# Two DMA queues for the first K weights, and a ScalarE square root for the first tile, at the start of a tuned attention and SwiGLU kernel

## The chip, the cores and the metric

One core of a Trainium2 chip. The metric is the device time of one execution in microseconds (us), lower is better; a kernel is run several times and the median is quoted. A ratio of two kernels is the mean time of the one's fast runs over the mean of the other's fast runs of the same rounds, so it is not quite the ratio of the quoted medians. A run counts as slow when it is over 1.5% above the fastest of its kernel. "Within noise" below always refers to the 95% interval of such a ratio, or to the spread of the same kernel between executions.

## The reference, cut to what matters

```python
xn = layernorm(x)                                   # x: 2048 tokens x 1024
q, k, v = split(xn @ wqkv)                          # wqkv: 1024 x 3072, 32 heads of 32
pq, pk = phi(q), phi(k)                             # phi(t) = where(t > 0, t+1, exp(t)) + 1e-6
kv  = sum over tokens of pk^T v                     # linear attention, not causal
s   = (pq kv) / (pq . sum pk) @ wo
g   = silu((silu(xn @ w_gate) * (xn @ w_up)) @ w_down)
out = x + s * g
```

The matrix products are nearly all of the time. What this case is about happens in the first ten microseconds: tile 0 (128 tokens) has to be loaded, normalised and transposed, and the first weights of K have to arrive, before TensorE can do anything useful.

## The kernel before: the parts concerned

The kernel is written as a list of operations, each with its engine, what it reads and writes, and an estimated duration. A planner (`schedule`) sorts them into one instruction stream for each engine; the stream is fixed when the kernel is built. Cuts are marked with `...`.

Tile 0 of x is loaded in two halves, one issued by SyncE and one by ScalarE (ACT). The weights all go out from SyncE:

```python
def wkv_load(w, j, k):            # w: 0 = K, 1 = V; j: half of the columns; k: half of the rows
    ap, r = kvblock(w, KB_OF[k, j])
    c0 = 1024 * (1 + w) + j * 512
    dma([], [r], ap, wqkv_v[:, 4 * k:4 * k + 4, c0:c0 + 512], dsem("wkv%d%d%d" % (w, j, k)), 512 * KB)
```

The order of the loads is tile 0, tile 1, then K (j=1, k=0), K (1, 1), K (0, 0), K (0, 1), tile 2, V (1, 0), V (1, 1), tile 3, V (0, 0), V (0, 1). I call the four K loads **blocks one to four** in this order, 512 KB each, and V (1, 0) the first V block.

The normalisation of one tile; in tiles 0 and 1 VectorE (DVE) writes the result in two halves:

```python
def ln_tile(i):
    ...
    oA = dve([...], [sA], lambda h: h.bn_stats(stats[:, j, 0, :], xa[:, 0:512]), 512)
    oB = dve([...], [sB], lambda h: h.bn_stats(stats[:, j, 1, :], xa[:, 512:1024]), 512)
    if i == 1:                                # tile 1's statistics wait for two steps of tile 0
        for o, q in zip((oA, oB), first):
            o.preds.add(q)
            q.succs.append(o)
    dve([sA, sB], [mvr], lambda h: h.bn_aggr(mv[:, j, :], stats[:, j, :, :]), 60)
    o0 = dve([mvr], [ver], lambda h: h.tensor_scalar(veps[:, j, :], mv[:, j, 1:2], EPS_LN, None, ALU.add), 60)
    if i == 0:
        first.append(o0)
    pool([ver, nh_r], [rsr], lambda h: h.tensor_tensor(rstd[:, j, :], veps[:, j, :], neg_half[:, :], ALU.pow), 0.56)
    ...
            o0 = dve([s.r, mvr, rsr], [...], lambda h, c=c: h.tensor_scalar(
                oa[:, c:c + n], xa[:, c:c + n], mv[:, j, 0:1], rstd[:, j, :], ALU.subtract, ALU.mult), n, 2.6)
    first.append(o0)
```

On TensorE (PE) the start is: 15 warm-up matmuls on zeros, eight transposes of tile 0, six small filler matmuls, four matmuls with block one, four with block two, eight transposes of tile 1, then blocks three and four and tile 1.

## Time and profile before

| what | value | from |
|---|---|---|
| median of three runs, their range | 712.48 us (711.99 to 712.89) | the times |
| span of the profiled execution | 710.5 us | the page |
| PE busy | 705.0 us, 99% | the page |
| transposes of tile 0 begin | 6.41 us | PE's timeline |
| PE starts on block one, block two, block three | 7.93, 9.33, 10.84 us | PE's timeline |
| last landing of block one, two, three, four | 7.79, 9.28, 10.79, 12.28 us | the landing records |
| last landing of the first V block | 14.48 us | the landing records |

How to read it: a DMA runs on 16 engines and each reports its landing separately, so a block has 16 landings and is usable at the last. The useful work of PE is fixed, and from 10.84 to 177 us it has almost no holes. So a landmark some way in measures what the start gains or loses. I use eight transposes near 125 us for this (called the transposes of the sums in the expectations below): the traces show 669 matmuls ahead of them, or 658 where 11 records are missing. In the kernel before they start at 124.96 us. (The chain of waits shows them 0.17 us later, 125.13, as it leaves out the overlap with the matmul ahead; some expectations use that reading.) The landmark does not tell the end of the kernel: after it PE has further holes, which differ between executions, and from PE's last matmul to the end of the span it takes 2.99, 3.69 and 3.00 us in three traces of this kernel, and up to 4.89 (e3).

### The profile page before, as it was taken

What the parts mean: (1) busy time and instruction counts of PE and PEld (TensorE: products, weight loads), DVE (VectorE), ACT (ScalarE), POOL (GpSimd) and SP (SyncE); (2) the same over time, 40 slices, a digit from 0 to 9 for tenths busy, and PEclk for the clock granted to TensorE, in tenths of its full rate; (3) what the DMA queues carried; (4) which work ended last, traced back from release to release, by engine and by line L of the source; (5) the groups of instructions that cost most, each with busy time, mean ns of one, the idle gap of its engine ahead of it and who ended that gap; (6) DMA issues with size and microseconds to landing.
All of it is one profiled execution on the core that took longest, in us unless ns stands there. A gap on an engine that the chain in (4) does not pass through costs nothing.

```text
span 710.5 us, 11436 instructions
## 1 busy us (share of the span) xinstructions
PE 705.0 (99%) x4181; PEld 388.5 (55%) x4181; DVE 631.4 (89%) x1533; ACT 423.3 (60%) x825; POOL 14.1 (2%) x35
## 2 busy tenths in 40 slices
PE   8999999999999999999999999999999999999997
PEld 4444445555555555556556455555555555565654
DVE  6999858989999999998958999999999999798863
ACT  4788765988679676664212157876886756531212
POOL 2111000000000000000000000000000000000000
PEclk9999999999999999999999999999999999999999
DMA  9744133346565353326498854323716241656663
GB/s 293 151 109 99 32 118 119 120 132 195 165 186 145 103 156 112 107 65 174 124 244 216 205 142 149 109 71 94 208 59 192 76 149 60 179 140 160 144 156 96
DMA packets 140871, 98.64 MB, mean 139 GB/s; under 512 B 34960, under 2 KB 137872, under 8 KB 140816
## 3 DMA queue, kind: packets, MB, share of 16 engines
q1 hardware_dynamic: 140528, 97.74, 49.5%
q8 instruction: 32, 0.52, 0.3%
q10 hardware_dynamic: 288, 0.20, 0.1%
q14 instruction: 23, 0.19, 0.1%
HBM read 77.59 MB, written 12.71 MB: 127 GB/s over the span
## 4 chain that ended last, share of the span: by engine, by line
PE 96%; DMA 2%; SPq 0%; DVE 0%; issue 0%; ACT 0%
PE ps L309 96%; DMA W<-in_B_w_up_dram 1%; DMA H<-in_A_wqkv_dram 1%; SPq L455 0%; DVE W L452 0%; PE ps L316 0%; DVE ps L452 0%; DVE TM L452 0%; SPq L757 0%; ACT TM L441 0%
## 5 line engine op out<-in xcount | busy, mean ns | idle before, releaser
L309 PE MATMUL ps<-X,W 128*128 128x512 f16 (+2 forms) x1372 | 288.7, 350 | 0.0
L441 ACT ACTIVATE TM<-ps 128x512 f16<-128x512 f32 (+3 forms) x386 | 202.6, 555 | 101.9 <-PE ps L309 99.0
L309 PE MATMUL ps<-H,W 128*128 128x512 f16 (+2 forms) x1096 | 218.2, 351 | 0.1
L309 PEld LDWEIGHTS ps<-X,W 128*128 128x128 f16 (+1 forms) x1372 | 132.4, 98 | 103.6 <-ACT H L441 1.0
L452 DVE TENSOR_TENSOR W<-W 128x1024 f16<-128x1024 bf16 (+5 forms) x412 | 183.1, 478 | 3.5 <-PE ps L309 2.1
L309 PEld LDWEIGHTS ps<-H,W 128*128 128x128 f16 (+1 forms) x1096 | 106.1, 98 | 94.8 <-DVE ps L452 0.6
L452 DVE TENSOR_TENSOR ps<-ps,TM 128x256 f32<-128x256 f32 (+1 forms) x250 | 131.5, 527 | 13.4 <-PE ps L309 10.0
L441 ACT ACTIVATE ps<-ps 128x512 f32<-128x512 f32 (+1 forms) x174 | 85.8, 494 | 90.3 <-PE ps L309 89.7
L441 ACT ACTIVATE H<-ps 128x512 f16<-128x512 f32 (+1 forms) x132 | 78.4, 606 | 38.3 <-PE ps L309 38.3
L309 PE MATMUL ps<-P,W 128*128 128x256 f16 (+1 forms) x516 | 99.5, 319 | 0.0
L452 DVE TENSOR_TENSOR H<-H 128x1024 f16<-128x1024 f16 (+5 forms) x126 | 71.2, 578 | 0.8 <-ACT H L441 0.4
L441 ACT ACTIVATE TM<-TM 128x512 f16<-128x512 f32 (+1 forms) x70 | 43.7, 630 | 45.5 <-DVE TM L452 45.3
L309 PEld LDWEIGHTS ps<-P,W 128*128 128x128 f16 (+1 forms) x516 | 50.2, 98 | 29.0 <-ACT TM L441 0.8
L309 PE MATMUL ps<-W 128*128 128x256 f16 (+1 forms) x330 | 61.8, 282 | 0.0
L452 DVE TENSOR_TENSOR H<-H,TM 128x512 f16<-128x512 f16 (+1 forms) x120 | 48.0, 417 | 8.5 <-ACT H L441 8.3
L452 DVE TENSOR_TENSOR TM<-ps,TM 128x512 f32<-128x512 f32 (+3 forms) x63 | 41.6, 660 | 13.6 <-PE ps L309 12.8
L309 PEld LDWEIGHTS ps<-W 128*128 128x128 f16 (+1 forms) x330 | 31.5, 98 | 31.7 <-DVE ps L452 1.2
L309 PE MATMUL ps<-H,X 128*128 128x512 bf16 (+1 forms) x150 | 35.0, 379 | 0.7 <-DMA H<-in_A_wqkv_dram 0.4
L452 DVE TENSOR_TENSOR TM<-TM 128x512 bf16<-128x512 f16 (+2 forms) x73 | 29.4, 412 | 6.4 <-ACT TM L441 4.5
L309 PE MATMUL ps<-H,P 128*128 128x512 bf16 (+1 forms) x110 | 26.8, 379 | 0.0
L452 DVE TENSOR_TENSOR H<-ps,TM 128x512 f16<-128x512 f32 (+1 forms) x35 | 24.0, 686 | 2.6 <-PE ps L309 1.7
L452 DVE TENSOR_TENSOR TM<-TM,W 128x512 f16<-128x512 f16 (+1 forms) x39 | 14.0, 363 | 11.5 <-ACT TM L441 11.4
(100 smaller groups left out, 397.7 us busy)
## 6 DMA issues: line engine op xcount, KB each, us to landing
W<-in_B_w_gate_dram SPq DMA_DIRECT2D x14, 1024.0 KB, 5.4
W<-in_B_w_up_dram SPq DMA_DIRECT2D x14, 1024.0 KB, 5.5
W<-in_B_w_down_dram SPq DMA_DIRECT2D x14, 896.0 KB, 6.2
H<-in_A_wqkv_dram SPq DMA_DIRECT2D x8, 512.0 KB, 8.1
H<-r_scratch SPq DMA_DIRECT2D x32, 128.0 KB, 3.8
W<-m_scratch SPq DMA_DIRECT2D x4, 1024.0 KB, 5.3
s_scratch<-TM SPq DMA_DIRECT2D x32, 128.0 KB, 2.0
TM<-in_A_x_dram SPq DMA_DIRECT2D x16, 256.0 KB, 3.5
```

The costliest lines, as they stand in the source:

```text
L309: last = h.matmul(o, l, r, start=st, stop=sp, skip_group_check=True)
L441: q = PL.op("act", reads, writes, lambda h: h.activation(o, i, func, **kw), nel(o) / (1000.0 if "bias" in kw or not isinstance(kw.get("sca ...
L452: return dve(reads, writes, lambda h: h.tensor_tensor(o, a, b, op), nel(o), 1.92 if fast else 0.96)
```

## The change

The intent: let the first weights land sooner by issuing two of the four K loads from ACT, and shorten the chain to tile 0's normalisation by replacing GpSimd's power with ACT's square root and VectorE's reciprocal. The core of the diff, shortened (`epsl` is a column filled with EPS_LN by VectorE at the start):

```diff
-        tab = ACT.Exp
+        tab = ACT.Sqrt                       # the planner's first activation table
...
         def wkv_load(w, j, k):
-            dma([], [r], ap, wqkv_v[...], dsem("wkv%d%d%d" % (w, j, k)), 512 * KB)
+            o = dma([], [r], ap, wqkv_v[...], dsem("wkv%d%d%d" % (w, j, k)), 512 * KB)
+            if (w, k) == (0, 0):             # K blocks one and three
+                beside.append(o)
...
-            o0 = dve([mvr], [ver], ... veps = var + EPS_LN ...)
             if i == 0:
+                o0 = act([mvr, el_r], [ver], veps[:, j, :], mv[:, j, 1:2], ACT.Sqrt, "sb", bias=epsl[:, :])
                 first.append(o0)
-            pool([ver, nh_r], [rsr], ... power ...)
+                dve([ver], [rsr], lambda h: h.reciprocal(rstd[:, j, :], veps[:, j, :]), 60)
+            else:
+                ... as before: veps on VectorE, power on GpSimd ...
...
                 for c in range(0, 1024, n):
-                    o0 = dve(... normalise half c ...)
+                    p0, o0 = o0, dve(... normalise half c ...)
+                    if c:
+                        o0.after = (p0,)     # second half of the normalisation behind the first
+                        p0.succs.append(o0)
...
         PL.schedule()
+        for o in beside:
+            o.eng = "act"
```

The queue is changed after planning, so the planner does not know of it. The Sqrt part does enter the plan.

More of the change, by code (lines that the diff above doesn't have):

```diff
@@ L375, in build_kernel @@
         epsc = sbt("epsc", [128, 1], F32)
+        epsl = sbt("epsl", [128, 1], F32)
         m_scr = nc.dram_tensor("m_scratch", [D, D], FP16)
@@ L569, in build_kernel @@
         wz = TM.at(0, 1 * KB, FP16)
+        el_r = named("el")
+        dve([], [el_r], lambda h: h.memset(epsl[:, :], EPS_LN), 60)
         wz_r = [TM.reg(0, KB // 4), TM.reg(KB // 4, 3 * KB // 4)]
@@ L762, in wkv_load @@
             c0 = 1024 * (1 + w) + j * 512
-            dma([], [r], ap, wqkv_v[:, 4 * k:4 * k + 4, c0:c0 + 512], dsem("wkv%d%d%d" % (w, j, k)), 512 * KB)
+            o = dma([], [r], ap, wqkv_v[:, 4 * k:4 * k + 4, c0:c0 + 512], dsem("wkv%d%d%d" % (w, j, k)), 512 * KB)
+            if (w, k) == (0, 0):
+                beside.append(o)
         xnslot = {}
-        first = []
+        first, beside = [], []
         def ln_tile(i):
@@ L779, in ln_tile @@
             dve([sA, sB], [mvr], lambda h: h.bn_aggr(mv[:, j, :], stats[:, j, :, :]), 60)
-            o0 = dve([mvr], [ver], lambda h: h.tensor_scalar(veps[:, j, :], mv[:, j, 1:2], EPS_LN, None, ALU.add), 60)
             if i == 0:
+                o0 = act([mvr, el_r], [ver], veps[:, j, :], mv[:, j, 1:2], ACT.Sqrt, "sb", bias=epsl[:, :])
                 first.append(o0)
-            pool([ver, nh_r], [rsr], lambda h: h.tensor_tensor(rstd[:, j, :], veps[:, j, :], neg_half[:, :], ALU.pow), 0.56)
+                dve([ver], [rsr], lambda h: h.reciprocal(rstd[:, j, :], veps[:, j, :]), 60)
+            else:
+                o0 = dve([mvr], [ver], lambda h: h.tensor_scalar(veps[:, j, :], mv[:, j, 1:2], EPS_LN, None, ALU.add), 60)
+                pool([ver, nh_r], [rsr], lambda h: h.tensor_tensor(rstd[:, j, :], veps[:, j, :], neg_half[:, :], ALU.pow), 0.56)
             o = xn_ring.take()
@@ L789, in ln_tile @@
                 for c in range(0, 1024, n):
-                    o0 = dve([s.r, mvr, rsr], [o.sub(2 * c, 2 * n).r], lambda h, c=c: h.tensor_scalar(
+                    p0, o0 = o0, dve([s.r, mvr, rsr], [o.sub(2 * c, 2 * n).r], lambda h, c=c: h.tensor_scalar(
                         oa[:, c:c + n], xa[:, c:c + n], mv[:, j, 0:1], rstd[:, j, :], ALU.subtract, ALU.mult), n, 2.6)
+                    if c:
+                        o0.after = (p0,)
+                        p0.succs.append(o0)
                 first.append(o0)
```

## The prediction

> **What bounds the kernel now.** I read the page first, for the busy shares and the chain that ended last; then that chain in order of time; then who waits; then the first 26 us engine by engine, because the chain sends me there.
>
> From the page (busy us, share, instructions), then three pieces of the chain in order of time (start us, us, what):
>
> ```profile
> PE 705.0 (99%) x4181; PEld 388.5 (55%) x4181; DVE 631.4 (89%) x1533; ACT 423.3 (60%) x825; POOL 14.1 (2%) x35
> PE 96%; DMA 2%; SPq 0%; DVE 0%; issue 0%; ACT 0%
> ...
> 2.20 7.09 DMA H<-in_A_wqkv_dram
> ...
> 10.84 114.29 PE ps L309 x624
> ```
>
> The tensor engine is busy 705.0 of 710.5 us, so 5.5 us is all that any change to waits can ever give back: 0.8% of the time. Stretch by stretch, PE lacks 1.8 us before 10.84, 0.14 us near 177 to 191, and 3.5 us in the tail after 705; elsewhere nothing. The change sits in the first stretch, so its direct worth is bounded by 1.8 us before anything else is said. The 1.04 us before PE's first instruction is not touched either.
>
> The waits of PE in the first 14 us (who, for whom, total, times, longest), then its own timeline there (start us, us, what, idle before):
>
> ```profile
> PE ps L309 <- DVE TM L571: 1.0, 1, 1.0
> PE ps L309 <- DMA H<-in_A_wqkv_dram: 0.4, 1, 0.4
> PE ps L309 <- ACT X L441: 0.3, 1, 0.3
> ```
>
> ```profile
> 1.04 5.30 PE L309 MATMUL ps<-TM 128*128 128x128 f16 x15 [1.04 <-DVE TM L571]
> 6.41 0.90 PE L316 MATMUL ps<-ident,W 128*128 128x128 f16 x8
> 7.14 0.50 PE L309 MATMUL ps<-TM 128*128 128x128 f16 x6
> 7.93 1.02 PE L309 MATMUL ps<-H,X 128*128 128x512 bf16 x4 [0.29 <-ACT X L441]
> 9.33 1.04 PE L309 MATMUL ps<-H,X 128*128 128x512 bf16 x4 [0.38 <-DMA H<-in_A_wqkv_dram]
> 10.21 0.61 PE L316 MATMUL ps<-ident,W 128*128 128x128 f16 x8
> ```
>
> The 15 warm-up matmuls are filler; real work begins with the transposes of tile 0 at 6.41 and runs without a hole from 10.84. Between lie the gaps that the change aims at. Matmuls of 512 columns start 0.215 us apart here, so the hole after the start at 8.58 is 9.33 - 8.80 = 0.53 us by starts (0.38 with modelled ends). After the transposes of tile 1 there is another of about 0.2 us, to 10.84.
>
> Matching each load's last landing with the instruction that waits for it gives the main point. The four K weight blocks (512 KB each; first columns-half 1 with k-half 0 and 1, then columns-half 0) land at 7.79, 9.28, 10.79 and 12.28; PE passes those waits at 7.82, 9.32, 10.83 and 13.22. The first V block lands at 14.48 and is waited for until 14.51, without a hole in the matmuls; the third V block lands at 18.17, wait passed at 18.20. So **the start is paced by one DMA stream to 18 us**, not only at the hole that the page shows.
>
> **What the Trainium skill says.** "DMA: Bandwidth & Descriptors", section "Issuing engines are not separate DMA queues": all issuing engines share the same 16 DMA engines, and a second issuer saves only issue time. The trace agrees that issue is small: SyncE's first weight issues take 0.43 to 0.64 us each, against 1.5 us between landings. The same page, "Queues, rings and completion order": each DMA engine takes turns between queues, packet by packet; the trace before has weights on one queue only, so no run shows it yet. "ScalarE: Activation LUTs", section "What ACT_TABLE_LOAD costs": 1283 ns for the load plus about 1380 ns of drain. The trace has eight loads of 1283 ns, but ACT's next instruction follows about 10 ns later (load 133.55, next 134.84): the drain is not seen as extra time, so I count 1.3 us. That section also gives 280 ns + 0.833 ns per element with a pointer bias; the trace's 128x128 activations take about 0.28 us.
>
> **The change, part by part.**
>
> (a) Standard deviation of tile 0. VectorE's and GpSimd's rows:
>
> ```profile
> 4.86 0.21 DVE L779 BATCH_NORM_AGGREGATE mv<-stats 128x2 f32<-128x12 f32 x1
> 5.11 0.15 DVE L780 TENSOR_SCALAR veps<-mv 128x1 f32<-128x1 f32 x1
> 5.35 0.56 POOL L783 TENSOR_TENSOR rstd<-veps,neg_half 128x1 f32<-128x1 f32 x1 [0.84 <-DVE veps L780]
> 5.94 0.73 DVE L790 TENSOR_SCALAR W<-W,mv,rstd 128x512 f16<-128x512 bf16 x2
> ```
>
> Today 5.07 to 5.94 = 0.87 us. New, an estimate: Sqrt with a pointer bias 0.28, reciprocal 0.17 (128x1 VectorE rows are 0.15, a small reciprocal elsewhere in the trace 0.20), three hand-offs of 0.03 to 0.04: 0.55 us. Saved 0.32. But PE is in order: its last warm-up starts at 5.70 and those start 0.43 apart, so PE is free only at 6.13, and the transposes can move from 6.41 to 6.13: **0.28 us at best**. A side effect goes the other way: half of tile 1's statistics ran free of charge in the power's shadow (5.30 to 5.98); now it falls behind the normalisation, and tile 1 may come 0.3 us later. That is covered if tile 0's matmuls on the third block stand beside it.
>
> (b) Table loads. The first load becomes Sqrt's, at the start where ACT idles to 6.84. A load for Exp is added, 1.3 us, after the four copies of tile 0 (end 8.16) and before the first Exp (10.40): 2.24 us idle there, so hidden with 0.9 us left. Worth 0.
>
> (c) Two queues. Issues now are at 1.73, 2.19, 2.74, 3.29. ACT is free at 1.18 after its half of x, so blocks one and three should go at about 1.2 and 1.65, and blocks two and four move up on SyncE to about 1.73 and 2.2: 0.5 to 1.1 us earlier. That is worth something only where the DMA engines had room. They had:
>
> ```profile
> 2.00:8.00 6.00, 5.64 (x26) 2.39 (x25) 3.99 (x10) 1.64 (x5) 2.72 (x12) 1.00 0.90 273
> 8.00:12.00 4.00, 3.60 (x22) 1.64 (x22) 2.58 (x6) 1.74 (x4) 0.34 (x1) 1.00 1.09 372
> ```
>
> The last two columns are the DMA share and GB/s. At 372 the first 6 us of traffic would take 4.4, so 1.6 us is the most that filling the stream gives. I count a third to a half, 0.5 to 0.8 us, as the low rate has a part that more queues need not mend: four of the 16 engines landed the first block at 7.71 to 7.79, ten by 5.8. Against it stands the turn-taking. In one queue block one ends after 1.0 MB; interleaved fairly with the rest of x and block two it ends after about 1.4 MB, block three after 2.4 in place of 2.0. At 372 GB/s, 0.4 MB is 1.1 us: order lost eats what start gained for the first and third blocks. Blocks two and four and all of V keep nearly their place and gain the shift whole.
>
> Sum: (a) 0.28 and both holes 0.53 + 0.2 give at most 1.0 us; the stream allows 0.5 to 0.8; turn-taking takes some back. I expect 0.6 us, and put the time at 711.8.
>
> **The rivals.** R1, the wait moves: PE begins 0.3 us earlier and stands before block one or three, late through turn-taking. For it: landing 7.79 against a use at 7.93, no slack. Time then 712.3 to 713. R2, the stream fills well, and everything to the third V block comes about 1 us earlier: 711.4. For it: the rate of 273; against: the stuck engines. R3, the transfer is hidden anyway: no, three waits pass within 0.04 us of a landing. R4, the order: the kernel's instruction order comes from a planner that models all engines; its starting table and its op list change, and the model does not know that two loads change queue. Another order for all 700 us can add or take holes; PE's holes after 11 us are 0.1 us each and few, so I allow 0.7 us either way. An engine becoming the new bound is out: ACT is at 60%, GpSimd at 2%.
>
> **Range and chances.** The three runs before spread 711.99 to 712.89. Uncertainty of the direct gain 0.5, of the order 0.7, of the median 0.4 make about 1 us together; I take 710.6 to 713.2. Two per cent is 14 us, over twice all the idle time of PE, so faster is near impossible; slower by that would need a broken order. Chances 0.01, 0.98, 0.01.
>
> **What would show it.** (a) right: ACT shows a Sqrt of about 0.28 us near 5.1, tile 0's normalisation starts near 5.6, transposes near 6.1. (b) right: a second table load between 7.9 and 9.5 with no PE wait behind it. (c) right: two queues carry the first MBs, a rate over 300 GB/s in 2 to 8 us, the first V block lands before 14.2. R1 right: PE's wait for weights grows. R4 right: holes elsewhere than before. The prediction is wrong if PE's busy time itself moves, or if the tail after 705 changes length.

## The result, and the profile after

The changed kernel took 711.84 us in the median of six runs (711.44 to 713.57); the kernel before, in six runs of the same comparison, 712.38 (710.95 to 713.33). The ratio is 0.9996 with a 95% interval of 0.9982 to 1.0011. The median fell where it was predicted, but the interval, 2 us wide, holds a gain of 1.3 us as well as a loss of 0.8. **The times alone don't say whether the change did anything.** So the rest is read from the traces.

PE in the first 14 us of the changed kernel (start us, us, instruction, idle before and what ended it):

```profile
6.60 0.72 PE L316 MATMUL ps<-ident,W 128*128 128x128 f16 x8 [0.27 <-DVE W L798]
7.16 0.50 PE L309 MATMUL ps<-TM 128*128 128x128 f16 x6
7.50 1.03 PE L309 MATMUL ps<-H,X 128*128 128x512 bf16 x4
9.04 1.02 PE L309 MATMUL ps<-H,X 128*128 128x512 bf16 x4 [0.52 <-DMA H<-in_A_wqkv_dram]
9.90 0.61 PE L316 MATMUL ps<-ident,W 128*128 128x128 f16 x8
10.35 5.82 PE L309 MATMUL ps<-H,X 128*128 128x512 bf16 x26
```

Compare with the same view before, in the prediction. The transposes of tile 0 are 0.19 us **later** than in that trace (two further traces of the kernel before, e1 and e12 below, have them at 6.44 and 6.67, so the path behind VectorE's statistics is the better measure), block one is started 0.43 us earlier, block two 0.29 us earlier, and the hole in front of block two has grown, from 0.38 to 0.52 by the modelled ends. At block three PE is 0.49 us ahead (10.35 against 10.84); a new hole of 0.16 us at 28.4 takes some of it back, and 0.29 us remain at the landmark: 124.67 against 124.96. PE's busy time is 705.0 us in both.

VectorE's and ACT's rows of the same stretch:

```profile
4.91 0.21 DVE L784 BATCH_NORM_AGGREGATE mv<-stats 128x2 f32<-128x12 f32 x1
5.48 0.16 DVE L788 RECIPROCAL rstd<-veps 128x1 f32<-128x1 f32 x1 [0.36 <-ACT veps L442]
5.56 0.67 DVE L778 BATCH_NORM_STATS2 stats<-W 128x6 f32<-128x512 bf16 x1
6.15 0.72 DVE L798 TENSOR_SCALAR W<-W,mv,rstd 128x512 f16<-128x512 bf16 x2
```

```profile
2.27 1.28 ACT L442 ACT_TABLE_LOAD   x1 [2.27 <-issue]
5.15 0.29 ACT L442 ACTIVATE veps<-mv,epsl 128x1 f32<-128x1 f32 x1 [1.60 <-DVE mv L784]
...
8.16 1.28 ACT L442 ACT_TABLE_LOAD   x1
10.10 0.60 ACT L442 ACTIVATE TM<-ps 128x512 f16<-128x512 f32 x1 [0.66 <-PE ps L309]
```

The Sqrt takes 0.29 and the reciprocal 0.16 us, and the reciprocal is done by 5.64. But between it and the normalisation (6.15) stands half of tile 1's statistics, 0.67 us. Before, that half ran in the shadow of GpSimd's power. By the planner's code, it found VectorE free for the short moment in which it counts the reciprocal's result as not yet ready (0.14 us), and put a long instruction there. The path from the end of the aggregate to the normalisation is now 6.15 - 5.12 = 1.03 us, against 0.87 before; it repeats, at 1.03 in five more traces with this order (e2, e4, e5, e6, e11) and at 0.86 to 0.87 in e1, e10 and e12 with the old one. The second table load, by contrast, is hidden as hoped: 8.16 to 9.44, and ACT still waits 0.66 us for PE.

The stream of loads (columns: stretch, its length, busy time of PE, PEld, DVE, ACT and POOL, clock, DMA share, GB/s), to be set against the two rows in the prediction:

```profile
2.00:8.00 6.00, 5.74 (x28) 2.25 (x27) 3.91 (x10) 2.65 (x6) 1.95 (x10) 1.00 1.00 335
8.00:12.00 4.00, 3.48 (x23) 1.59 (x22) 2.91 (x8) 3.00 (x5) 0.56 (x1) 1.00 1.10 355
```

In 2 to 8 us the rate rose from 273 to 335 GB/s. The last landings by the landing records: block one 5.89 (before 7.79), block two 8.90 (9.28), block three 8.24 (10.79), first V block 12.58 (14.48). So the stream as a whole is nearly 2 us earlier, and block three even overtakes block two; yet block two, the one that PE stands before, came only 0.38 us earlier.

One more thing is in this trace: the chain that ended last passes through late landings of a DMA transpose and of gate weights, with holes in PE from 407 to 416 us.

```profile
402.00:418.00 16.00, 14.97 (x81) 7.40 (x80) 13.43 (x34) 7.04 (x13) 0.00 (x0) 1.00 0.91 188
```

PE lacks 1.03 us in these 16 (1.6 us by the starts of the matmuls). That eats the start's gain several times over, and this execution, 713.57 us, was the slowest of the six. Whether these holes belong to the change is one of the questions for the experiments.

### The profile page after: what moved, and what is told of

Read it like the earlier page. It is cut to its first block, busy times and chain, and to the rows that moved or that the text cites. A ratio compares the mean times of both kernels' runs of the same rounds, so it can differ in the third digit from the quotient of the medians.

```text
span 711.8 us, 11445 instructions
## 1 busy us (share of the span) xinstructions
PE 705.0 (99%) x4181; PEld 387.3 (54%) x4181; DVE 630.9 (89%) x1534; ACT 424.7 (60%) x827; POOL 12.8 (2%) x34
## 3 DMA queue, kind: packets, MB, share of 16 engines
HBM read 77.59 MB, written 12.71 MB: 127 GB/s over the span
## 4 chain that ended last, share of the span: by engine, by line
PE 93%; DMA 3%; DVE 3%; issue 0%; SPq 0%; ACT 0%; DVEq 0%
PE ps L309 93%; DVE W L453 1%; DMA W<-in_B_w_gate_dram 1%; DMA H<-in_A_wqkv_dram 1%; DMA TM<-TM 1%; DVE TM L453 1%; DVE X L453 0%; DVE ps L453 0%; PE ps L316 0%; DVE P L453 0%; SPq L456 0%; SPq L760 0%; ACT TM L442 0%; SPq L1621 0%; DVEq L301 0%
## 5 line engine op out<-in xcount | busy, mean ns | idle before, releaser
L453 DVE TENSOR_TENSOR TM<-TM 128x512 bf16<-128x512 f16 (+2 forms) x73 | 29.3, 414 | 7.0 <-ACT TM L442 4.3
```

Of the source, the lines that this page charges most:

```text
L453: return dve(reads, writes, lambda h: h.tensor_tensor(o, a, b, op), nel(o), 1.92 if fast else 0.96)
```

## The experiments

Two theories stood at the outset. **The queues**: the start is paced by the landings, and two queues bring them forward. **The Sqrt path, or the new order of instructions**: these carry a gain or a loss of their own. And behind both, whether a single trace of each kernel can be trusted: so the first two runs change nothing.

### e1: the kernel before, once more

No edit.

> The kernel before, unchanged, profiled a second time. It tells whether the stall of four DMA engines (first K block landing spread over 5.30 to 7.79 us, last landing 7.79) belongs to the kernel or to that one execution. Theory A (one issuing queue makes it): the first K block lands again after 7 us, the first V block near 14.5, PE's first K matmul near 7.9, and the transposes of the sums (chain piece of PE at 125.13) within 0.1 of 125.1. Theory B (an accident of that execution): the first K block lands near 5.9, the first V block near 12.6 to 13. The time ratio to the kernel before is 1.000 within 0.001; its distance from 1 is the noise of this method.

Measured: ratio to the same kernel 0.9982, interval 0.9969 to 0.9994 (712.0 against 713.27 us in the median). **The same program compared with itself came out faster, clear of its own interval.** In the trace, from the chain in order of time (start us, us, what):

```profile
2.20 6.39 DMA H<-in_A_wqkv_dram
...
8.63 1.04 PE ps L309 x4
...
10.14 114.33 PE ps L309 x624
```

Block one landed at 6.86 (7.79 in the first trace), block two at 8.59 (9.28), the first V block at 13.78 (14.48), and the landmark stands at 124.30 against 124.96. Neither theory fits as put: the spread of block one between DMA engines is still there (first landing 5.40, last 6.86), but smaller. What follows: one execution of the kernel before differs from another by 0.66 us at the landmark, more than the 0.29 us that the first pair of traces showed as the change's gain. Single traces can't be compared for such amounts; landings and holes over several can.

### e2: the changed kernel, once more

No edit.

> The changed kernel, unchanged, profiled a second time. Theory: the gain at the start is 0.3 us and repeats (PE's start on the second K block near 9.0, piece of PE transposes at 124.8), and the 1.7 us of PE holes between 407 and 416 us do not repeat, as they came from one late landing of gate weights; then the whole is 0.3 to 0.8 us under the kernel before, ratio 0.9989 to 0.9996. Rival: the new instruction order brings the holes at 407 to 416 every time; then the ratio is 1.000 to 1.002.

Measured: median 712.03 us, against 712.0 of e1 in the same rounds; the ratio to the kernel before, 0.998 (0.9967 to 0.9994), is no better than e1's. All four kernels e1 to e4 share one set of nine runs of the kernel before, so e1 against the others is the fairer comparison. The holes at 407 to 416 did not come back. The same stretch, about 1 us earlier in this execution:

```profile
401.00:417.00 16.00, 16.00 (x90) 8.56 (x88) 14.66 (x36) 6.97 (x13) 0.00 (x0) 1.00 0.73 188
```

PE is full, and the other traces with this order (e4, e5, e6, e11) have no such holes. So they were an accident of one execution, in which several landings were late: the gate weights took 8.07 us from issue (5.92 in e2), and two DMA transposes 7.08 and 6.31 (4.58 and 3.73). The landmark is at 124.35, block one landed at 6.01, block two at 8.57, block three at 9.85, the first V block at 12.71.

### e3 and e4: each part alone

e3 takes the kernel before and adds only the two queues. Its instruction order is the old one, as the queue is changed after planning.

```diff
+            if (w, k) == (0, 0):
+                beside.append(o)
...
+        for o in beside:
+            o.eng = "act"
```

> Only the two queues, with the instruction order, the first tile's power on GpSimd and all else of the kernel before. Theory: the whole of the start's gain is the queues': first K block lands near 5.9 and no longer counts, transposes of tile 0 stay at 6.4, PE starts its first K matmul near 7.4 and the second block, landing near 8.9, releases it at 9.0, so 0.3 us are won: same as the changed kernel. Rival: the Sqrt part carries something; then PE is later at the second block than in the changed kernel by 0.2 us or more.

e4 is the changed kernel without these lines.

```diff
-        for o in beside:
-            o.eng = "act"
```

> Only the Sqrt and reciprocal with the new instruction order; all K loads on one queue. Theory: normalisation of tile 0 starts at 6.15 as in the changed kernel, 0.2 us later than before, since half of tile 1's statistics slips between; the first K block decides (landing 7.8 if the stall repeats) and PE's second K block starts at 9.3: gain 0.0, within 0.1 us. Rival: the quicker standard deviation gains 0.2 to 0.3 us by itself, transposes of tile 0 at 6.1 to 6.2.

Measured, e3: ratio 0.999 (0.9977 to 1.0002); block one at 5.95, block two at 9.07, block three at 8.82, first V block at 12.77; PE starts block two at 9.12; landmark 124.59. In e3 tile 0's transposes come at 6.58, not the 6.4 expected: VectorE waits 0.21 us for tile 1, whose load now shares the engines with block one and lands at 5.41 (4.25 in the first trace before). e4: ratio 0.9993 (0.998 to 1.0005); block one at 7.39, block two at 8.87, first V block at 14.05; PE starts block two at 9.00; landmark 124.71; and the normalisation of tile 0 is again behind half of tile 1's statistics, 1.04 us after the aggregate's end (6.37 against 5.33).

What follows: the earlier first and V blocks belong to the queues alone, since e3 has them and e4 has not. The Sqrt path by itself makes tile 0 later, not earlier, by 0.16 us after the aggregate. And neither part brings block two forward: 8.59 to 9.28 in e1 and the first trace, 8.87 in e4, all with one queue; 8.57 to 9.07 in the three traces with two. PE waits before block two in all of them, and this gate has not moved (in e2 it holds PE by 0.13 us only, and the chain that ended last passes through tile 0's normalisation instead). One more difference follows the instruction order: the traces with the changed kernel's order (its first, e2, e4, and e5, e6 and e11 below) have a hole of 0.16 to 0.17 us in PE near 28 us (27.9 to 29.3), and none with the old order has it.

Behind block two the traces agree so well that single ones can be compared. From the start of tile 1's transposes to block three PE takes 0.63 to 0.64 us in the three traces of the kernel before, 0.55 in e4, and 0.45 in the changed kernel's two and in e3: **the queues close the hole before block three, a gain of 0.18 us.** From PE's start on block two to the landmark it is 115.63 to 115.67 us before, 115.47 with the queues alone, 115.71 with the Sqrt alone and 115.63 and 115.65 with both. So the queues' 0.18 us is real, and the hole near 28 us, which comes with the new order, takes it back.

### Why block two stays: e5 and e6

Theory: block three, put on ACT's queue, takes turns with block two on SyncE's, so the bytes which PE needs last get the engines that block two needs now. The trace of the changed kernel by queue says how much (queue and kind, packets, MB, share of the 16 engines; q10 is ACT's queue, q1 SyncE's), first for 2 to 5.9 us, then for 5.9 to 8:

```profile
q10 hardware_dynamic: 879, 0.87, 65.1%
q1 hardware_dynamic: 287, 0.39, 30.3%
```

```profile
q1 hardware_dynamic: 448, 0.46, 67.6%
q10 hardware_dynamic: 300, 0.29, 42.3%
```

By 5.9 us ACT's queue had moved over twice what SyncE's had, and SyncE's, whose 0.39 MB are its half of tile 0 and tile 1, was only beginning on block two. In the second stretch block three takes 0.29 MB of the 0.75 that moved. e5 leaves block one on ACT and sends block three back:

```diff
-            if (w, k) == (0, 0):
+            if (w, j, k) == (0, 1, 0):
```

> The changed kernel, but only the first K block goes out on ACT's queue; the third goes back to SyncE's, behind the second. Theory: the change left the start where it was because the third block, put on ACT's queue, takes turns with the second, which is the one PE waits for (second block landing 8.6 to 9.1 with one queue and with two). With the third behind it, the second has all engines once the first is through at 5.9: some 0.45 MB left at 340 GB/s, so it lands at 7.2 to 7.6; PE starts it right behind the first, at 8.4 to 8.6, without a hole; transposes of the sums at about 124.1 to 124.2. Rival: the second block's landing is set by its issue or by its own packets, and stays at 8.6 to 9.0, PE's start on it at 8.7 to 9.1.

e6 tries another pairing: block two follows block one on ACT's queue, three and four go to SyncE's.

```diff
-            if (w, k) == (0, 0):
+            if (w, j) == (0, 1):
```

> The changed kernel with the first and second K block on ACT's queue, the third and fourth on SyncE's. Theory of sharing: the second block now takes turns with the rest of x and the third block, and lands where the third did in the changed kernel, 8.2 to 9.9: no clear gain, PE's start on it 8.4 to 9.9. Rival (ACT's queue is simply quicker): it lands before 7.8.

Measured, e5: block two lands at 7.65; in 5.9 to 8 us SyncE's queue has the engines alone:

```profile
q1 hardware_dynamic: 731, 0.73, 109.3%
```

and PE runs from block one into block two without a stop:

```profile
7.34 0.50 PE L309 MATMUL ps<-TM 128*128 128x128 f16 x6
7.67 1.89 PE L309 MATMUL ps<-H,X 128*128 128x512 bf16 x8
9.40 0.68 PE L316 MATMUL ps<-ident,W 128*128 128x128 f16 x8
```

The eight matmuls in one row are blocks one and two; the second four start at 8.53. Landmark 124.20. With block two in time, the chain that ended last now runs through tile 0's normalisation: PE stands 1.10 us before tile 0's transposes. Its time, 711.87 us in the median, is not to be told from the kernel before (ratio 1.0003, 0.9987 to 1.002; one of six runs took 715.09).

e6: block two lands at 9.84, later than in any other run, and block three, now on SyncE's queue, at 8.56. PE starts block two at 9.97 and the landmark falls back to 125.61. So ACT's queue is not the quicker one as such. With two weight blocks waiting behind the first, one on each queue, both are late: in the changed kernel's two traces, e3 and e6 they end at 8.24 to 9.85, and which of the two ends first changes. The sharing theory holds; the rival, that a block's landing is set by its own packets or its queue, falls (e6 is one trace, and e5 is repeated below).

The packet records say the same in bytes. (I added up the packets that had ended when a block's last part landed; no view of the profile prints this sum.) By block two's landing 1.95 to 2.13 MB had moved in the kernel before and e4, 2.19 to 2.42 in the changed kernel's two traces, e3 and e7, 2.63 in e6, and 1.83 to 1.91 in the five traces with block one alone on ACT. So the changed kernel has the quicker stream, but puts block two 0.1 to 0.5 MB further back in it; e5 has the quicker stream and leaves block two its place.

### Giving VectorE the right order: e7

e7 is the changed kernel with both halves of tile 1's statistics held behind tile 0's normalisation.

```diff
-                for o, q in zip((oA, oB), first):
+                for o, q in zip((oA, oB), (first[-1], first[-1])):
```

> The changed kernel with both halves of tile 1's statistics held until tile 0's normalisation is done. Theory: the normalisation then follows the reciprocal within 0.1 us (5.65 to 5.85 in place of 6.15 to 6.35), the transposes of tile 0 start at 6.15 to 6.35, the first K matmul at about 7.1, but the second K block lands when it did (8.6 to 9.1) and PE starts it then: the hole grows by the 0.45 us won, and the time gains nothing. Rival: the start moves as a whole, second block at 8.3.

Measured, one look (a single run, its clock 1.0): VectorE, then PE:

```profile
5.70 0.16 DVE L788 RECIPROCAL rstd<-veps 128x1 f32<-128x1 f32 x1 [0.36 <-ACT veps L442]
5.90 0.73 DVE L798 TENSOR_SCALAR W<-W,mv,rstd 128x512 f16<-128x512 bf16 x2
```

```profile
7.26 1.03 PE L309 MATMUL ps<-H,X 128*128 128x512 bf16 x4
8.65 2.04 PE L309 MATMUL ps<-H,X 128*128 128x512 bf16 x8 [0.36 <-DMA H<-in_A_wqkv_dram]
```

The path from the aggregate's end (5.34) to the normalisation is 0.56 us, 0.47 less than in the first trace of the changed kernel. PE is at block one at 7.26, and then waits for block two, which lands at 8.51. Landmark 124.44, between the changed kernel's own 124.35 and 124.67. So the quicker path by itself only lengthens the wait, as theory said. The plan also moved the matmuls of block three ahead of tile 1's transposes here (the row of eight).

### Both mends, and a third look: e8 to e12

e8 and e9 are one kernel with the edits of e5 and e7 together. e10 is the kernel before with the placement of e5 alone, no Sqrt. e11 repeats e5, e12 the kernel before.

> Both mends together: only the first K block on ACT's queue, and tile 1's statistics behind tile 0's normalisation. Theory: first K matmul at about 7.1, second block landing 7.2 to 7.6 and started at about 8.0, so PE is 0.7 to 1.0 us ahead of the changed kernel there, if the third block (used right behind it in this order) is in by 8.9; transposes of the sums at 123.7 to 124.0. The time should then be about 0.8 us under the changed kernel, ratio to the kernel before 0.998 to 0.999, which this method may not separate from 1.

> Both mends together, profiled once more because the profile of the first run fell into an execution with the clock at 0.655. Theory as before: second K block lands at 7.3 to 7.7, PE's first K matmul at 7.0 to 7.3 and the second block right behind it at 7.9 to 8.2, no hole over 0.1 us; the third block (about 9.0) is wanted at about 8.9 in this order, so a hole of up to 0.2 us may stand there; transposes of the sums at 123.7 to 124.1. Rival: something else holds PE at 8.6 or later.

> The kernel before with a single edit: the first K block on ACT's queue, everything else (power on GpSimd, instruction order) as it was. Theory: the queue placement alone is worth the gain: second block lands at 7.3 to 7.7, PE starts it at 8.3 to 8.5 without a hole, transposes of the sums at 123.9 to 124.2. Rival: the gain of the single block on ACT needs the Sqrt part; then PE starts the second block at 8.7 or later.

> The changed kernel with only the first K block on ACT, profiled a second time, for the spread between executions. Theory: the second block lands within 0.3 us of 7.65 again, PE's start on it 8.3 to 8.6, transposes of the sums 124.0 to 124.3. Rival: it was luck; then it lands at 8.5 or later.

> The kernel before, profiled a third time, on the same chip as the mends. Theory: with one queue the second block lands between 8.5 and 9.4, the first V block between 13.6 and 14.6, transposes of the sums 124.3 to 125.0. Rival: it lands at 8.0 or earlier, and the mends' gain is only the spread between executions. Its time ratio to itself shows the noise once more, within 0.002 of 1.

e8's profile fell into an execution of 1061.06 us with a granted clock of 0.655; its four other runs took 711.59 to 712.51. From it I take only the landings, which the clock does not touch visibly (block two 7.47). Everything else is from e9, PE's row first, in the same view as above:

```profile
6.10 0.72 PE L316 MATMUL ps<-ident,W 128*128 128x128 f16 x8 [0.38 <-DVE W L798]
...
7.00 1.89 PE L309 MATMUL ps<-H,X 128*128 128x512 bf16 x8
9.04 1.04 PE L309 MATMUL ps<-H,X 128*128 128x512 bf16 x4 [0.16 <-DMA H<-in_A_wqkv_dram]
...
10.77 3.40 PE L309 MATMUL ps<-H,X 128*128 128x512 bf16 x15 [0.25 <-DMA H<-in_A_wqkv_dram]
```

The normalisation follows the aggregate by 0.55 us (5.08 to 5.63), tile 0's transposes start at 6.10, blocks one and two run through from 7.00, and now block three, landing at 8.99, is the gate at 9.04: the hole by starts is 8.50 to 9.04, of which 0.32 us is waiting, more than the 0.2 I had allowed. A second hole stands before block four (landing 10.50): its first matmul is one of the missing records, but its weight load starts at 10.54, so the true hole is about 0.2 us and not the 0.4 that the row at 10.77 suggests. Landmark 124.03. All together; "landing" is the last landing, times in us:

| kernel | trace | block one lands | block two lands | first V block lands | PE starts block two | landmark |
|---|---|---|---|---|---|---|
| before | first, e1, e12 | 7.79, 6.86, 7.30 | 9.28, 8.59, 8.80 | 14.48, 13.78, 14.01 | 9.33, 8.63, 8.85 | 124.96, 124.30, 124.52 |
| Sqrt alone | e4 | 7.39 | 8.87 | 14.05 | 9.00 | 124.71 |
| changed | first, e2 | 5.89, 6.01 | 8.90, 8.57 | 12.58, 12.71 | 9.04, 8.70 | 124.67, 124.35 |
| its queues alone | e3 | 5.95 | 9.07 | 12.77 | 9.12 | 124.59 |
| only block one on ACT | e5, e11 | 5.90, 6.26 | 7.65, 7.76 | 12.84, 12.96 | 8.53, 8.63 | 124.20, 124.30 |
| the same, no Sqrt | e10 | 6.18 | 7.68 | 12.88 | 8.62 | 124.08 |
| both mends | e9 | 5.98 | 7.49 | 12.68 | 7.86 | 124.03 |

The rows of "only block one on ACT" do not overlap with the others in block two's landing: 7.47 to 7.76 in five traces, against 8.51 to 9.28 in eight with the other placements (9.84 in e6). e1 to e4, e5 to e8 and e9 to e12 ran on three different chips; the separation holds within each of the last two (7.47 and 7.65 against 8.51 and 9.84; 7.49 to 7.76 against 8.80). At the landmark the kernels with block one alone on ACT stand at 124.03 to 124.30, the kernel before at 124.30 to 124.96: the means are 124.15 of four and 124.59 of three, 0.44 us apart. The ranges touch, and the four are three different kernels, so the landing is shown and the size of the gain at the landmark is not. At PE's last matmul the two groups overlap: 706.15 to 706.79 against 706.55 to 707.56.

In time it is not resolved. e9, e10, e11 and e12 ran in the same rounds: 711.54, 711.54, 711.64 and, for the unchanged kernel before, 711.48 us in the median. e9's ratio, 0.9986 (0.9973 to 0.9998), and e10's, 0.9985 (0.9971 to 0.9999), look like gains, but e1, the same program on both sides, reads 0.9982 and e12 0.9991 (0.9978 to 1.0004). e11 reads 0.9989 (0.9976 to 1.0001), e8's four fast runs 0.9993 (0.998 to 1.0006). So no version here is shown to beat either kernel by its time. If one had to be kept, e10's single edit has the earlier landing and leaves the planner's order alone, so that it keeps the 0.18 us behind block two (124.08 - 8.62 = 115.46).

## Why the prediction was right or wrong

**The time was right, and part of the working was not.** 711.8 was predicted and 711.84 measured, but with an interval that holds anything from a gain of 1.3 to a loss of 0.8 us this agreement proves little: it is luck, as the gain it was built on is not seen. The bound was right and did the work: 5.5 us of PE idle in all, so "within 2%" was near certain.

**The gain of 0.6 us at the start**: over the traces it is smaller. Mean landmark 124.59 of three for the kernel before, 124.51 of two for the changed one: 0.08 us, far below the 0.66 us between executions. So most of the first pair's 0.29 us is spread between executions: the kernel before stood 0.37 above its own mean there. The expected gain was too large, and where it was to come from failed in two steps. Of the two holes that it was summed from, the 0.2 before block three did close, and the hole near 28 took it back; the 0.53 before block two stayed, at 0.21 to 0.54 in the kernel before and 0.13 and 0.68 in the changed one.

**Step (a), "Saved 0.32", failed.** Its costs were right: Sqrt 0.29 for the 0.28 predicted, reciprocal 0.16 for 0.17, and with the intruder held back the whole path is 0.55 to 0.56 us (e7, e9) for the 0.55 predicted. What failed is that the prediction placed the displaced half of tile 1's statistics behind the normalisation; it stands in front of it, and the path grew to 1.03 us. The diff's own line shows how: tile 1's first statistics are released by the Sqrt, at the same moment as the reciprocal. The prediction took it that the planner would then put the more urgent normalisation first; it fills the short wait before it with a long instruction. The bound of 6.13 for the transposes was one execution's too: in e9 the warm-up was done earlier, and they start at 6.10 after waiting 0.38 us for VectorE.

**Step (b), table loads worth 0, was right**: 1.28 us each, the second hidden with 0.66 us to spare where 0.9 was predicted.

**Step (c), the stream gains "0.5 to 0.8 us", was too small, and it went to the wrong block.** The first V block lands 1.1 to 1.9 us earlier with the change (12.58 and 12.71, against 13.78 to 14.48), and 2 to 8 us carry 335 GB/s in place of 273 to 290. But of the turn-taking I had the direction reversed: "order lost eats what start gained for the first and third blocks. Blocks two and four and all of V keep nearly their place and gain the shift whole." Blocks one and three gained most, and block two kept its landing. In bytes: block one was to end after 1.4 MB in place of 1.0, and 1.26 and 1.30 were measured with the change, but 1.31 to 1.58 without it; with one queue its landings are spread (5.30 to 7.79 us in the first trace), and by the last of them other loads had moved bytes too, so it had no early place to lose. Block two was said to keep its place; it went from between 1.95 and 2.13 MB back to 2.20 and 2.33. The prediction's own fair sharing would have said so: by it block two ends after about 1.8 MB in place of 1.5, a sum that was done for blocks one and three alone. And all three signs that were named for (c) came true, as none of them was block two's landing.

**Rival R1, "the wait moves"**, is nearest to what happened, with the other block: PE's wait before weights grew from 0.4 to 0.5 us in the first pair of traces. In the second traces the hole by starts is 0.23 us (e1) and 0.13 (e2). R2's stream came true for V (the first and third V blocks 1.1 to 1.9 us earlier), but not for block two, and so without the time that it promised. R3 (hidden anyway) was rightly refused: e5 shows that moving one landing moves PE. R4 (the order elsewhere) was given 0.7 us; what the new order is shown to cost is the 0.16 us near 28. The larger holes are not its doing: those at 407 to 416 did not repeat in e2, and the kernel before had 0.14 us missing near 177 to 191 in its first trace and none in e1 and e12. Of the two signs of being wrong, PE's busy time did not move; the tail after PE's last matmul did, from 2.99 to 3.36 us, but it moves as much in the kernel before against itself (3.69 in e1), so that sign could not tell anything.

**What stays open.** Why, with one queue, block one's 16 landings are spread over 1.5 to 2.5 us, I can't say: no view shows what holds those engines. Why ACT's queue got twice the bytes in the first trace (0.87 to 0.39 MB) and e3, and not in e2 (0.67 to 0.60), is open as well. In these two traces, and in e8 and e9, ACT's half of tile 0 landed before SyncE's, and tile 1, on SyncE's queue, only at 5.29 to 5.87 us; in the other six traces with two queues the halves landed the other way round, and tile 1 at 4.49 to 4.86. That the one causes the other is not shown. A rival to the second queue was not tried: to put block one ahead of tile 1 on SyncE's own queue. And whether the best variant saves some 0.4 us in time would need far more runs than were spent.

## What to carry to other kernels

Putting transfers on a second queue does not only start them earlier: it also decides what they compete with, so put there the one transfer that is needed next and nothing needed later, and name beforehand the landing of the block that the engine actually waits for. When a long wait is shortened, look at what the instruction order used to do inside it. And before a gain of a tenth of a per cent is believed, run the unchanged kernel against itself: here it read 0.9982, and its own start moved by 0.66 us.

## What the Trainium skill lacked or had wrong

- "DMA: Bandwidth & Descriptors", section "Rules for kernel authors", says of spreading DMAs over issuing engines for bandwidth that it doesn't help and only saves issue time. In the first microseconds here it did: 273, 290 and 278 GB/s in 2 to 8 us for the kernel before, 282 in e4, against 335, 335 and 342 with two queues (the changed kernel twice, e3) and 325 to 338 with block one alone on ACT. Earlier issue alone does not explain it: with one queue all four K loads were issued by 4.0 us, and yet 4 to 6 us carried 201 to 244 GB/s, against 379 to 384 in the changed kernel and e3. In 8 to 12 us the rule holds: 354 to 355 with two queues, 361 to 372 with one.
- The same page, section "Queues, rings and completion order", describes taking turns between queues by packets, but not what share a queue gets. The runs show it uneven and changing: by 5.9 us, 0.87 MB on ACT's queue and 0.39 on SyncE's in the changed kernel's first trace, 0.67 and 0.60 in its second.
- No page gives the spread of one load's 16 landings at the start of a kernel: with one queue block one's landings ran from 5.30 to 7.79 us, 5.40 to 6.86, 5.44 to 7.30 and 5.44 to 7.39; with block one on ACT's queue the same spread was 0.3 to 0.8 us.
- "ScalarE: Activation LUTs", section "What ACT_TABLE_LOAD costs", adds about 1380 ns of drain to each load. The 1283 ns load is confirmed in every trace; the drain is not seen as time between instructions: in the kernel before, one load starts at 133.55 us, about 0.02 after the activation ahead of it ends, and the next activation follows at 134.84.
